# Weaving the first blocked chunk of a Fourier mixing kernel into its last plain steps

## The chip, the cores and the metric

The kernel runs on one core of a Trainium2 chip. The metric is the device time of one execution in microseconds, and before the change its median over three runs is 1843.8 us (1842.21 to 1844.92). A profile of one execution tells where the time goes; its own time is given further down, because here it is very different from the runs' median.

The engines have short names in all rows: PE is TensorE (matmuls), PEld its weight loads, DVE is VectorE, ACT is ScalarE, POOL is GpSimd and SP is SyncE, which issues nearly all DMAs here.

## The reference

```python
# x: (8, 3008, 256), w_in: (256, 2048), w_out: (2048, 256), all float32
X = np.fft.fft(x, axis=1)                   # along the 3008 positions
X = np.fft.fft(X, axis=2)                   # along the 256 features
h = X.real.reshape(24064, 256) @ w_in       # up projection
g = np.maximum(0.01 * h, h)                 # leaky relu
out = g @ w_out                             # down projection
```

## The kernel before

**The units.** The Fourier transform along the positions is done by folds (sums and differences of mirrored rows, on DVE and POOL) and matmuls with cosine and sine tables. Its result lies in `mix_sb` (a cosine and a sine part) and `nb_sb` (a separate term, "nyquist" in the code), for one *unit* at a time: a batch and a parity of the frequency, 16 units in all. The transform along the features is not done at all at run time: it is folded into the weights (`fold_w_in` makes `wf` from w_in and a table). Frequencies come in pairs of plus and minus, which differ only in the sign of the sine part. So an up projection makes a cosine and a sine product for a block of 128 of the 2048 hidden features, and DVE makes their sum and their difference.

**Two ways to compute.** The first 502 columns of unit 0 are computed as two *plain* column blocks of 251 columns each. For these there are 16 plain steps, `steps[0..15]`, each a pair (column block `j`, two feature blocks `f`). A plain step has an up half (`raised`, four matmuls into a cosine and a sine bank that `ring("up")` hands out; `activate`, four DVE operations and a leaky relu on ACT) and a down half (`down_plain`, eight matmuls into the PSUM banks that collect the output). While they run, the weights arrive and are converted from 64-bit words on DVE (`convert_on(old, new)` finishes one piece and begins the next: `w3[0]`, `w3[1]` are parts of w_in, `o4` to `o7` of w_out), and POOL adds weights to one another (`sum_weights`, 18 sums), which the second way needs.

All other columns are computed as 31 *chunks*, with a fast blocked product for the down projection: fewer matmuls, more additions. Chunk 0 is the last 250 columns of unit 0, the others have 376 or 378. A chunk has 16 *ups*. For each, ACT writes the nyquist term into the cosine bank (`Chunk.seed`), PE adds the cosine product to it and makes the sine product in a second bank (`Chunk.up`), ACT copies the cosine bank to SBUF, DVE makes sum and difference out of copy and sine bank (`Chunk.hidden`), and one up later ACT applies the leaky relu. There are two pairs of banks, `cos_ps[f % 2]` and `sin_ps[f % 2]` (the names in rows end in `a` and `b`), so that one up can begin while the other is read. After the ups come 28 sums of hidden values (`SUMS`, on POOL and partly on DVE), 26 products of four matmuls each (`PRODUCTS`, into three banks), 34 additions on DVE (`COMBINED`), and the output's stores on SP. Hidden values lie in 28 *slots* of 764 words each in `block_sb`; in the plain stage the same tile holds weights, buffers and plain hidden values.

**The order.** The order on each engine is the order in which the program issues, written out by hand. First come the plain steps: for step `at`, a conversion, then the up half of step `at`, then the down half of step `at - 2`:

```python
for at, old, new in ((8, o4, o5), (9, o5, w3[0]), (10, w3[0], w3[1]), (11, w3[1], o6),
                     (12, o6, o7), (13, o7, None), (14, None, None), (15, None, None)):
    ...
    up(*steps[at])
    if at == 11:
        fold_w_in(3 * WN, WN, w3)
    ...
    down_plain(*steps[at - 2])
    if at in SUM_WEIGHTS:          # {10: (0, 1, 2), 13: (3,)}
        ...sum_weights(last)
```

Then `rest()` makes one list of events for all chunks, sorted by a due time that counts in ups: the ups of chunk `t` at 16t + 1.2 + f, its sums at hand-written times `SUMS_AT`, its products from 16t + 18.1 on, 6.5 to an up. In step 0 to 15 of this list `start_work(r)` also issues what is left of the start: the last two down halves (r = 0, 1), the nyquist rows (r = 2) and two transforms `dft_direct` (r = 4, 7) that prepare later units. Work on the next batch comes from the generator `work()`: the load of x from step 9 (`yield 9, 0`), its folds `folds_of_x` from step 14. `wait_for_gate` lets an operation of POOL wait for an operation of DVE, where both would use SBUF at once.

The lines to know in rows of the kernel before: L880 up and L915 down matmuls of a plain step, L893 to L895 its DVE operations, L1063 seed, L1068 up matmuls, L1074 copy, L1081 sum and difference, L1329 leaky relu, L1098 a chunk's sums, L1115 its products, L576 to L595 conversions, L655 sums of weights, L934 and L936 folds of x, L693 matmuls of the transform.

## Time and profile before

| | before |
|---|---|
| median of the runs | 1843.8 us (1842.21 to 1844.92) |
| profiled execution | 3897.31 us |
| its span | 3895.5 us |
| granted clock of TensorE | 1.00 |
| PE busy | 3889.6 us |
| DVE, ACT, POOL busy | 1459.8, 1132.7, 1053.7 us |
| instructions | 27101 |
| HBM read, written | 62.12 MB, 24.72 MB |

The profiled execution took 2.11 times the median. Its rows give durations and order of every instruction; the median is what the change is measured by. Busy times are sums over the whole span. In a row of the trace the columns are: start in the span and duration in microseconds, engine, line, operation, output and inputs with their shapes; what is in brackets is idle time of the engine before the instruction, and what ended it. In a view by stretches the first column is a stretch of the span, then its length, then the busy time and the instructions of each engine, the granted clock, and what the DMA engines did.

### The profile page before, as it was taken

The page shows a single profiled execution, that of the slowest core. Times are in us where ns is not written, and L with a number is a line of the kernel's source. Part 1 is how long each engine was busy: PE and PEld are TensorE (multiplying, and loading weights), DVE is VectorE, ACT ScalarE, POOL GpSimd, SP SyncE. Part 2 cuts the span into 40 slices and gives each one's busy share as a digit, 9 for nine tenths or more (in the row PEclk, how much of TensorE's full clock was granted, in tenths as well). Part 3 has the DMA queues.
Part 4 walks back from the last instruction along what each step waited for, and adds up shares of the span by engine and source line. Part 5 has one row for each costly group of instructions (what it writes and reads, how often), then busy time and mean ns, then how long its engine had stood idle before and what let it go on. Part 6 is the DMA issues. An engine that isn't in the chain of part 4 may idle for free.

```text
span 3895.5 us, 27101 instructions
## 1 busy us (share of the span) xinstructions
PE 3889.6 (100%) x9424; PEld 2809.1 (72%) x9424; DVE 1459.8 (37%) x3212; ACT 1132.7 (29%) x2298; POOL 1053.7 (27%) x595
## 2 busy tenths in 40 slices
PE   9999999999999999999999999999999999999999
PEld 5667777777777777777777777777777777777778
DVE  4435333343334433333333433334343343333233
ACT  2234232232323323233222322223222232222220
POOL 0113222322222322232222323222223222232222
DMA  3110000000000000000001001000010000000000
GB/s 115 51 37 31 32 13 13 34 14 28 12 13 33 16 27 11 14 33 16 34 6 34 11 15 34 16 24 12 14 34 16 27 11 13 11 16 8 4 6 14
DMA packets 65897, 88.61 MB, mean 23 GB/s; under 512 B 10064, under 2 KB 53456, under 8 KB 65760
## 3 DMA queue, kind: packets, MB, share of 16 engines
q1 hardware_dynamic: 65616, 86.88, 6.9%
q8 instruction: 74, 1.21, 0.1%
q14 instruction: 63, 0.52, 0.0%
q10 hardware_dynamic: 144, 0.00, 0.0%
HBM read 62.12 MB, written 24.72 MB: 22 GB/s over the span
## 4 chain that ended last, share of the span: by engine, by line
PE 100%; DVE 0%; issue 0%; POOL 0%; DVEq 0%; POOLq 0%
PE sum_psc L1115 22%; PE sum_psa L1115 17%; PE sum_psb L1115 17%; PE sin_psb L1068 9%; PE cos_psa L1068 9%; PE sin_psa L1068 9%; PE cos_psb L1068 9%; PE dft_ps L693 2%; PE sum_psa L915 1%; PE sum_psc L915 1%; PE sum_psb L915 1%; PE dft_ps L915 1%; PE sum_psa L1359 0%; PE cos_psb L880 0%; PE cos_psa L880 0%; PE sin_psb L880 0%
## 5 line engine op out<-in xcount | busy, mean ns | idle before, releaser
L1098 POOL TENSOR_TENSOR block<-block 128x752 f32<-128x752 f32 (+2 forms) x551 | 1025.3, 1871 | 2641.9 <-DVE xt L936 559.5
L1081 DVE TENSOR_TENSOR block<-cos,sin_psa 128x376 f32<-128x376 f32 (+2 forms) x496 | 246.7, 539 | 1165.5 <-PE sin_psa L1068 1028.2
L1115 PEld LDWEIGHTS sum_psc<-block,wt 128*128 128x128 f32 x1736 | 529.3, 311 | 186.0 <-issue 171.8
L1115 PE MATMUL sum_psc<-block,wt 128*128 128x188 f32 (+2 forms) x1736 | 660.1, 552 | 0.0
L1081 DVE TENSOR_TENSOR block<-cos,sin_psb 128x376 f32<-128x376 f32 (+2 forms) x496 | 246.8, 539 | 1062.3 <-PE sin_psb L1068 1018.6
L1115 PE MATMUL sum_psa<-block,wt 128*128 128x188 f32 (+2 forms) x1736 | 640.4, 552 | 0.0
L1115 PEld LDWEIGHTS sum_psa<-block,wt 128*128 128x128 f32 x1736 | 520.4, 309 | 125.0 <-issue 108.8
L1329 ACT ACTIVATE block<-block 128x376 f32<-128x376 f32 (+4 forms) x714 | 421.7, 620 | 0.0
L1068 PE MATMUL cos_psa<-mixc,wf 128*128 128x376 f32 (+2 forms) x496 | 391.6, 906 | 0.0
L1068 PE MATMUL sin_psb<-mixs,wf 128*128 128x376 f32 (+2 forms) x496 | 391.0, 903 | 0.0
L1068 PE MATMUL cos_psb<-mixc,wf 128*128 128x376 f32 (+2 forms) x496 | 388.8, 879 | 0.0
L1068 PE MATMUL sin_psa<-mixs,wf 128*128 128x376 f32 (+2 forms) x496 | 387.4, 879 | 0.0
L1074 ACT COPY cos<-cos_psb 128x376 f32<-128x376 f32 (+2 forms) x248 | 116.5, 470 | 916.1 <-PE cos_psb L1068 916.1
L1115 PE MATMUL sum_psb<-block,wo 128*128 128x188 f32 (+2 forms) x992 | 378.0, 552 | 0.0
L1115 PEld LDWEIGHTS sum_psb<-block,wo 128*128 128x128 f32 x992 | 301.3, 310 | 101.0 <-issue 92.2
L1115 PEld LDWEIGHTS sum_psb<-block,wt 128*128 128x128 f32 x992 | 299.8, 309 | 101.4 <-issue 92.2
L1115 PE MATMUL sum_psb<-block,wt 128*128 128x188 f32 (+2 forms) x992 | 364.8, 553 | 0.0
L1074 ACT COPY cos<-cos_psa 128x376 f32<-128x376 f32 (+2 forms) x248 | 116.5, 470 | 845.0 <-PE cos_psa L1068 845.0
L1098 DVE TENSOR_TENSOR block<-block 128x752 f32<-128x752 f32 (+2 forms) x317 | 338.1, 1068 | 2.6 <-POOL block L1098 2.1
L1068 PEld LDWEIGHTS sin_psa<-mixs,wf 128*128 128x128 f32 x496 | 157.3, 317 | 176.4 <-issue 174.8
L1068 PEld LDWEIGHTS sin_psb<-mixs,wf 128*128 128x128 f32 x496 | 141.5, 285 | 191.6 <-issue 191.1
L1115 PE MATMUL sum_psc<-block,wo 128*128 128x188 f32 (+2 forms) x744 | 272.3, 550 | 0.0
(222 smaller groups left out, 2648.1 us busy)
## 6 DMA issues: line engine op xcount, KB each, us to landing
xt<-in_x_dram SPq DMA_DIRECT2D x28, 1024.0 KB, 5.5
out_dram<-part SPq DMA_DIRECT2D x176, 94.0 KB, 1.7
out_dram<-part SPq DMA_DIRECT2D x64, 94.5 KB, 1.7
tabe<-in_seq_tab_dram SPq DMA_DIRECT2D x29, 190.0 KB, 2.6
nb<-nyq_dram SPq DMA_DIRECT2D x23, 188.0 KB, 3.7
block<-in_w_in_dram SPq DMA_DIRECT2D x8, 512.0 KB, 5.5
block<-in_w_out_dram SPq DMA_DIRECT2D x8, 512.0 KB, 4.5
xt<-in_first_x_dram SPq DMA_DIRECT2D x4, 768.0 KB, 8.6
```

Of the source, the lines that this page charges most:

```text
L693: nc.tensor.matmul(o, lhsT=still, rhs=moving, start=(i == 0), stop=(i == 3), skip_group_check=True)
L915: nc.tensor.matmul(sums[j][d][:, r * n : (r + 1) * n], lhsT=wo[:, fs[h] // 4, fs[h] % 4, d], rhs=a[r][h], start=(f == 0 and r == 0 and h = ...
L1068: nc.tensor.matmul(bank[:, 0 : self.w], lhsT=wf[:, i, f * P : (f + 1) * P], rhs=columns_of(mix_sb[i], self.u, self.j, self.w), start=(i == ...
L1074: nc.scalar.copy(copy, cos[:, 0 : self.w])
L1081: nc.vector.tensor_tensor(block.row(to, g, self.n), x, y, op=op)
L1098: ins = (engine or nc.gpsimd).tensor_tensor(self.value(16 + i), xa, ya, op=ALU.add if sign > 0 else ALU.subtract)
L1115: nc.tensor.matmul(to, lhsT=weight(w)[:, g], rhs=self.value(v)[:, g], start=(first and at == 0), stop=(last and g == 3), skip_group_check= ...
L1329: nc.scalar.activation(to, to, ACT.Lrelu)
```

## The change

The change has several parts, all between plain step 8 and the second chunk.

- **Chunk 0's ups beside plain steps 12 to 15.** The loop over the plain steps ends at step 11, and `rest()` begins there. The up halves of steps 12 to 15 are issued in the event list at r = 0, 2, 4, 6, and the down halves of steps 10 to 15 in halves of four matmuls at the r of `PLAIN_DOWN`. Between them stand the ups of chunk 0. For these to have PSUM banks at the same time, the first `EARLY` = 14 ups of chunk 0 all use the pair `cos_ps[0]`, `sin_ps[0]`, and the plain steps (and the transforms at r = 9, 11, 13) use the pair `cos_ps[1]`, `sin_ps[1]`. A seed is then issued one up ahead in place of two. The leaky relu of a moved plain step is put off to the next up.
- **Narrow slots.** Hidden values of chunk 0 lie in 16 slots of 4x126 words in the first 8064 words of `block_sb`; the ordinary slots over them come free as these are dropped. The output tiles of the plain steps move to `part_sb`.
- **Conversions and sums of weights.** The conversion of o6 with o7's begin is issued at r = 0, the end of o7 at r = 2. `sum_weights(0)` and `(1)` come after step 11's up half and wait, through the gate, for the end of w3[1]'s conversion; `(2)` and `(3)` come at r = 2.
- **Other preparation.** The nyquist folds come at step 9 (before: step 14), the nyquist rows at r = 9 (2), the folds for `dft_direct` at r = 5, 7, 8, 10 (plain step 14), `dft_direct` itself at r = 11 and 13 (4 and 7). The load of x is issued at step 14 (9), its folds at step 16 (14).
- `FIRST_DOWN` = 18.1 and `FIRST_SHARE` = 1.0 have the values that stood there before.

The number and the shapes of the matmuls are the same in both kernels. The diff, cut to its core:

```diff
+EARLY = 14
+FIRST_DOWN = 18.1
+RF = 126
+FIRST_SHARE = 1.0
+DIRECT = (11, 13)
+WORK_FROM = 14
+FOLDS_FROM = 16
...
-    lay_out(part_sb, 0, (("cos", 3, WN),))
+    lay_out(part_sb, 0, (("cos", 3, WN), ("out", 2, 2 * WN)))
...
-                nc.gpsimd.tensor_tensor(weight(8 + i), weight(x), weight(y), op=ALU.add if sign > 0 else ALU.subtract)
+                wait_for_gate(nc.gpsimd.tensor_tensor(weight(8 + i), weight(x), weight(y), op=ALU.add if sign > 0 else ALU.subtract))
...
+    steps[-2:] = steps[-1], steps[-2]
...
-    def activate(j, f):
+    def activate(j, f, later=None):
...
-        nc.scalar.activation(g, g, ACT.Lrelu)
+        if later is None:
+            nc.scalar.activation(g, g, ACT.Lrelu)
+        else:
+            later.append([g])
...
-            self.free = set(range(SLOTS))
+            self.under = {SLOTS + i: {4 * RF * i // SS, (4 * RF * (i + 1) - 1) // SS} for i in range(16)}
+            self.free = set(range(SLOTS)) - set().union(*self.under.values())
...
+        def half(self, f):
+            return 0 if self is every[0] and f < EARLY else f % 2
+
         def seed(self, f):
-            nc.scalar.activation(cos_ps[f % 2][:, 0 : self.w], columns_of(nb_sb, self.u, self.j, self.w), ACT.Copy, scale=wn[:, f : f + 1])
+            nc.scalar.activation(cos_ps[self.half(f)][:, 0 : self.w], columns_of(nb_sb, self.u, self.j, self.w), ACT.Copy, scale=wn[:, f : f + 1])
 
         def up(self, f):
-            cos, sin = cos_ps[f % 2], sin_ps[f % 2]
+            cos, sin = cos_ps[self.half(f)], sin_ps[self.half(f)]
...
-        yield 9, 0
+        yield WORK_FROM, 0
         load_x(1, 0)
-        yield step_of(1, -2), 0
+        yield FOLDS_FROM, 0
         folds_of_x(0)
...
-        rings["dft"] = [0, [misc_ps, *sums_ps]]
+        rings["up"] = [0, [cos_ps[1], sin_ps[1]]]
...
+        def seed_next(at):
+            if at < EARLY:
+                seed(at + 1)
+            if at + 2 > EARLY:
+                seed(at + 2)
...
-    SUM_WEIGHTS = {10: (0, 1, 2), 13: (3,)}
+    PLAIN_UP = {0: 12, 2: 13, 4: 14, 6: 15}
+    PLAIN_DOWN = {0: (10, 0), 1: (10, 1), 3: (11, 0), 4: (11, 1), 5: (12, 0), 7: (12, 1), 8: (13, 0), 9: (13, 1),
+                  10: (14, 0), 12: (14, 1), 15: (15, 0), 17: (15, 1)}
 
     def start_work(r):
-        if r < 2:
-            down_plain(*steps[14 + r])
+        if r == 0:
+            convert_on(o6, o7)
+        if r in PLAIN_UP:
+            raised(*steps[PLAIN_UP[r]])
+            activate(*steps[PLAIN_UP[r]], later=waiting)
+        if r in PLAIN_DOWN:
+            at, half = PLAIN_DOWN[r]
+            down_plain(*steps[at], halves=(half,))
         if r == 2:
+            convert_on(o7, None)
+            sum_weights(2)
+            sum_weights(3)
+        if r in (5, 7):
+            part = (r - 5) // 2
+            fold_halves(t, part, 0, slice(0, 2 * FI))
+            evens.append(Direct(t[:, part, 0, :, part * P : (part + 1) * P], part, even_tables[part], 0))
+        if r in (8, 10):
+            evens[(r - 8) // 2].fold_odd(t[:, (r - 8) // 2, 1, 0:2, 0:P])
+        if r == 9:
+            rings["dft"] = rings["up"]
             nyq_t = nyquist_tile()
...
-        if r in (4, 7):
-            dft_direct((r - 4) // 3)
+        if r in DIRECT:
+            dft_direct(DIRECT.index(r))
...
-            for at, old, new in ((8, o4, o5), (9, o5, w3[0]), (10, w3[0], w3[1]), (11, w3[1], o6), (12, o6, o7), (13, o7, None), (14, None, None), (15, None, None)):
-                if old is not None:
-                    convert_on(old, new)
+            for at, old, new in ((8, o4, o5), (9, o5, w3[0]), (10, w3[0], w3[1]), (11, w3[1], o6)):
+                done = convert_on(old, new)
...
                 if at == 11:
                     fold_w_in(3 * WN, WN, w3)
+                    gate.append(done)
+                    sum_weights(0)
+                    sum_weights(1)
...
-                if at in SUM_WEIGHTS:
-                    for last in SUM_WEIGHTS[at]:
-                        sum_weights(last)
-                if at == 14:
+                if at == 9:
                     fold_nyquist(0)
                     nyq = Rows(nya[:, 0], [nyz], 0, 0)
...
-                    for part in range(2):
-                        fold_halves(t, part, 0, slice(0, 2 * FI))
-                        evens.append(Direct(t[:, part, 0, :, part * P : (part + 1) * P], part, even_tables[part], 0))
-                    for part in range(2):
-                        evens[part].fold_odd(t[:, part, 1, 0:2, 0:P])
             rest()
```

More of the change, by code (lines that the diff above doesn't have):

```diff
@@ L587, in end @@
             if not self.f64:
-                nc.vector.tensor_copy(self.dst, self.raw)
-                return
+                return nc.vector.tensor_copy(self.dst, self.raw)
             hi = self.word(I32, 1)
@@ L594, in end @@
             v.scalar_tensor_tensor(power_i, in0=hi, scalar=-(2**31), in1=power_i, op0=ALU.bitwise_and, op1=ALU.bitwise_or)
-            v.scalar_tensor_tensor(man, in0=man, scalar=2.0**-20, in1=power, op0=ALU.mult, op1=ALU.mult)
+            return v.scalar_tensor_tensor(man, in0=man, scalar=2.0**-20, in1=power, op0=ALU.mult, op1=ALU.mult)
     parts = []
@@ L610, in convert_on @@
             new.begin()
-        old.end()
+        return old.end()
     def load_w_in(f0, n, blocks=(0, 1)):
@@ L903, in out_tile @@
     def out_tile():
-        return ring("o")[:, 0 : 4 * CW].rearrange("p (a n) -> p a n", a=2)
+        return ring("out")[:, 0 : 4 * CW].rearrange("p (a n) -> p a n", a=2)
     def down_plain(j, f, halves=(0, 1)):
@@ L1009, in drop @@
         def drop(self, i):
-            self.free.add(i)
+            if i in self.under:
+                freed = self.under.pop(i)
+                self.free |= freed - set().union(*self.under.values())
+            else:
+                self.free.add(i)
         def place(self, i, n):
+            if i >= SLOTS:
+                return block_sb[:, (i - SLOTS) * 4 * RF : (i - SLOTS + 1) * 4 * RF].rearrange("p (g n) -> p g n", g=4)[:, :, 0:n]
             return block_sb[:, i * SS : i * SS + 4 * RS].rearrange("p (g n) -> p g n", g=4)[:, :, 0:n]
         def row(self, r, g, n):
+            if r[0] >= SLOTS:
+                all_of = block_sb[:, 0 : 64 * RF].rearrange("p (i n) -> p i n", n=4 * RF)
+                return all_of[:, r[0] - SLOTS : r[-1] + 1 - SLOTS, g * RF : g * RF + n]
             all_of = block_sb.rearrange("p (i n) -> p i n", n=SS)
@@ L1071, in up @@
             if g == 0:
-                self.at.update(zip(range(4 * k, 4 * k + 4), block.take_four()))
+                self.at.update(zip(range(4 * k, 4 * k + 4), block.take_four() if self is not every[0] else range(SLOTS + 4 * k, SLOTS + 4 * k + 4)))
             copy = cos_sb[:, f % 2, 0 : self.w]
@@ L1243, in work @@
                 yield from transform(u + 1)
-    every = []
+    every, waiting = [], []
     def rest():
@@ L1257, in rest @@
             for m in range(4 * len(PRODUCTS)):
-                events.append((16 * t + DOWN_FROM + m / PER_STEP, 2, t, m))
+                events.append((16 * t + (DOWN_FROM if t else FIRST_DOWN) + m / PER_STEP, 2, t, m))
         for r in range(16 * count + 18):
@@ L1269, in seed @@
                 every[ups[at][0]].seed(ups[at][1])
-        us = [0.0, 0.0]
+        def seed_next(at):
[3 more added lines that the diff above has]
+                seed(at + 2)
+        us, now = [0.0, 0.0], [1.0]
         def some(pool):
-            us[pool], us[1 - pool] = min(us[pool], 0.3) + (ON_VECTOR, ON_POOL)[pool], us[1 - pool] - 100.0
+            us[pool], us[1 - pool] = min(us[pool], 0.3) + (ON_VECTOR, ON_POOL)[pool] * now[0], us[1 - pool] - 100.0
             for part in every:
@@ L1295, in go_on @@
                 empty = -1
-        after, waiting = [0], []
+        after = [0]
         seed(0)
-        seed(1)
         for _, kind, t, i in events:
             if kind == 0:
-                if t == 0:
-                    start_work(i)
-                elif t < count:
+                start_work(16 * t + i)
+                now[0] = FIRST_SHARE if 16 * t + i < 34 else 1.0
+                if 0 < t < count:
                     rings["dft"] = [0, [misc_ps]]
@@ L1325, in rest @@
                 made = part.up(i)
-                seed(16 * t + i + 2)
+                seed_next(16 * t + i)
                 folds.emit_copies()
@@ L1503, in tile_fnet_leaky_relu @@
                 up(*steps[at])
-                if at == 11:
-                    fold_w_in(3 * WN, WN, w3)
-                if at == 8:
-                    down_plain(*steps[at - 2], halves=(1,))
-                else:
-                    down_plain(*steps[at - 2])
-                if at in SUM_WEIGHTS:
-                    for last in SUM_WEIGHTS[at]:
-                        sum_weights(last)
-                if at == 14:
+                if at == 9:
                     fold_nyquist(0)
@@ L1518, in tile_fnet_leaky_relu @@
                     nyq_of.append(nyq)
-                    for part in range(2):
-                        fold_halves(t, part, 0, slice(0, 2 * FI))
-                        evens.append(Direct(t[:, part, 0, :, part * P : (part + 1) * P], part, even_tables[part], 0))
-                    for part in range(2):
-                        evens[part].fold_odd(t[:, part, 1, 0:2, 0:P])
+                if at == 11:
+                    fold_w_in(3 * WN, WN, w3)
+                    gate.append(done)
+                    sum_weights(0)
+                    sum_weights(1)
+                if at == 8:
+                    down_plain(*steps[at - 2], halves=(1,))
+                else:
+                    down_plain(*steps[at - 2])
             rest()
```

## The prediction

> **What bounds the kernel now.** I read the page's first two parts, then stretches of the stage that the change touches, then single engines in time. The page says that TensorE is all:

> ```profile
> span 3895.5 us, 27101 instructions
> ...
> PE 3889.6 (100%) x9424; PEld 2809.1 (72%) x9424; DVE 1459.8 (37%) x3212; ACT 1132.7 (29%) x2298; POOL 1053.7 (27%) x595
> ```

> The profiled execution took 3897.3 us: its span of 3895.5 and 1.8 around it. The runs' median is 1843.8, 0.473 of that. So the first question is which engine is slow in the profile. This row and the next start 3.63 us apart, for four matmuls of 251 columns (each stands as two records):

> ```profile
> 241.60 3.79 PE L915 MATMUL dft_ps<-block,wo 128*128 128x251 f32 x8
> 245.23 1.16 PE L1068 MATMUL cos_psa<-mixc,wf 128*128 128x250 f32 x2
> ```

> That is 3.6 ns a column. The program has 4712 matmuls; the shapes of the PE groups add up to 1,061,690 columns, and the median divided by them is 1.74 ns, with every stall in it. [...] By the row, TensorE never waits and a change of order is worth nothing: 3897 stays 3897. [...] I take 1.667 ns for TensorE and the trace's durations for the rest. Stretches: steps 9 to 11, steps 12 to 15 with the last downs ("P"), the first chunk's ups ("D"), the second chunk's ups ("E"):

> ```profile
> core 0: us, PE busy (x) PEld busy (x) DVE busy (x) ACT busy (x) POOL busy (x), PEclk, DMA share, GB/s
> 127.70:186.60 58.90, 58.90 (x114) 33.88 (x112) 22.33 (x36) 13.52 (x18) 9.45 (x7) 1.00 0.08 21
> 186.60:245.20 58.60, 58.60 (x129) 38.89 (x128) 12.96 (x25) 7.41 (x13) 15.74 (x21) 1.00 0.03 9
> 245.20:288.40 43.20, 43.20 (x106) 28.50 (x105) 19.08 (x57) 23.53 (x54) 0.68 (x1) 1.00 0.21 70
> 288.40:330.00 41.60, 41.60 (x119) 29.78 (x118) 21.20 (x39) 19.90 (x38) 14.38 (x11) 1.00 0.18 61
> ```

> P has 64 matmuls of 251 columns: 26.8 us of TensorE against 13.0 of DVE and 7.4 of ACT. D has 11,794 columns, 19.7 us, against 23.5 of ACT: there ACT is the bound. In P TensorE is the bound and ACT idles; the change lays the two over each other. How ACT fills D:

> ```profile
> 280.36 0.37 ACT L1074 COPY cos<-cos_psb 128x250 f32<-128x250 f32 x1 [0.34 <-PE cos_psb L1068]
> 280.76 0.47 ACT L1063 ACTIVATE cos_psb<-nb,wn 128x250 f32<-128x250 f32 x1
> 281.17 0.60 ACT L1329 ACTIVATE block<-block 128x500 f32<-128x500 f32 x1
> ...
> 285.41 0.62 ACT L1329 ACTIVATE block<-block 128x500 f32<-128x500 f32 x1
> 285.94 0.34 ACT L1074 COPY cos<-cos_psa 128x250 f32<-128x250 f32 x1
> ```

> From start to start a copy takes 0.40, a seed 0.41, a leaky relu 0.53: 1.34 us an up, where TensorE needs 500 columns, 0.83 us.

> **The change part by part.**

> **1. First chunk's ups among the last plain steps.** Before: P 26.8. Then D: ups 0 to 7 stand among the nyquist rows and two butterflies (3,794 columns, 6.3 us, beside 8 ups of 0.83), and with the last output copy and the butterflies' adds on DVE ahead of some ups' adds, ACT comes to the copy of up 8 at 15. Then it goes on by 1.34: six ups, a fold copy (0.51), the copy of up 14 and E's first seed (0.9), so the first up of E starts at 24.5. (ACT's busy sum of 23.5 and 0.7 at the start give nearly the same.) P and D are 51.3 us.
> After: the same columns, 27,858, are 46.4 us, with ACT at 31 and DVE at 32 beneath. But the first 14 ups share one pair of banks. Between two ups there is mostly half a down step (4x251 columns, 1.67 us) or a plain up (1.67). The next cos matmul needs copy and seed, 0.15 + 0.40 + 0.47 = 1.0 us after the last one; the next sin matmul needs DVE's pair of adds (0.74). Both fit into 1.67. Going up by up I find three places where they don't: at step 2 DVE stands in the end of o7's conversion (0.61 + 0.71 + 0.65) before the adds of up 1, TensorE waits 1.3; after the nyquist rows (1.5 us on DVE) 0.2; between ups 12 and 13, where nothing lies between, 0.6 and 0.4. Sum 2.5, so 48.9. Gain 2.4. The 0.15 from a matmul's end to its reader isn't in this trace; 0 would give 0.5 us more, 0.4 would stall half of the ups by 0.2, 1.5 less.

> **2. Folds of x two steps later.** Before, DVE enters E with a queue:

> ```profile
> 292.23 1.00 DVE L1081 TENSOR_TENSOR block<-cos,sin_psa 128x378 f32<-128x378 f32 x2
> 293.14 0.68 DVE L934 TENSOR_TENSOR xt<-xt,dft_ps 128x512 f32<-128x512 f32 x1
> 293.74 1.42 DVE L1098 TENSOR_TENSOR block<-block 128x500 f32<-128x500 f32 x1
> ```

> Even here nothing lies between them. At full speed the first fold copy is there 23.0 us into D; then three folds, two sums and a fold (0.60 each) and two ups' adds (0.74 each), with 0.1 of waiting, bring up 15's adds to 28.2. E's second up needs that bank and could have gone on at 26.6 (24.5, a first up of 756 columns and a product before it, its own cos half): 1.6 us are lost. After, five of the fold operations (0.60 each, start to start) come behind the adds, and two halves of a down step have given DVE and POOL time: that loss is gone, gain 1.6. They come back in E: by the built orders DVE has 41.7 us under the 16 ups of E where it had 39.3 (512 elements 0.60, 250 elements 0.33), and TensorE 39.0. From the seventh up the two orders nearly agree. I take 0.7 lost of the 2.4 (0 to 2.4), because the next three ups are lighter.
> The x loads, issued at step 14 instead of 9, wait on SP behind two output stores. They may start 41.2 us in and are first needed by ACT at 48.4: 7.2 us for what the trace shows landing in 5.2. Cost 0; without that cover ACT stands still with the output copies behind it, for which the first product waits.

> **3. Sums of weights behind the conversions.** Before, seven sums on POOL (from 146.68, 9.4 us) meet the conversion of w3[0]:

> ```profile
> 149.99 0.68 DVE L893 TENSOR_TENSOR block<-part,sin_psa 128x502 f32<-128x502 f32 x1 [0.89 <-PE sin_psa L880]
> ...
> 152.10 1.49 DVE L576 TENSOR_SCALAR block<-block 128x512 int32<-128x512 int32 x1
> ...
> 162.78 0.42 DVE L576 TENSOR_SCALAR wo<-block 128x512 int32<-128x512 int32 x1
> ```

> Four DVE instructions of that conversion take 5.5 us (from 151.17 to 156.71) where the next one's take 2.0 (162.17 to 164.17). At full speed, counted from the end of up 9: its adds 1.35, the conversion 2.6 + 3.5, step 10's activation 2.05, w3[1]'s conversion 2.6, together 12.1. TensorE has 24 matmuls of 251 (10.0) and the first half of a fold (0.85) until it needs w3[1]: at 10.85. It waits 1.3. After, the sums wait for o6's start and w3[1]'s end; the gain is 1.3. [...] But TensorE doesn't wait for o6: step 12's activation begins at 1.6 instead of 1.0 and the next plain up in its bank comes at 5.85. So 1.3 stays, from 0 to 1.7. Later sums (11 of 1.27) come under adds out of PSUM, and two folds of 0.95 that may double; their readers have 0.5 us to spare. Behind them POOL's first chunk sum is free at 25 us and needed at 45.

> **4. Taken at nothing.** Narrow slots: the same operations and elements (from -0.1 to +0.1 us each, I take 0). Nyquist folds moved up to step 9 on POOL, 2.5 us, under POOL's long idle time; without it ACT's four 0.29 us turns would hold back a conversion. Output tiles in part: the same copies and stores, of which the chunk's adds no longer have to wait.

> Sum: 2.4 + 1.6 - 0.7 + 1.3 = 4.6 us. 1843.8 - 4.6 = 1839.2. In the profiled execution, where TensorE hides all this, I expect no change from 3897.3.

> **The rivals.** *A: more than that.* If ACT and DVE wait longer for each other in D than I counted (0.2 us for each of 16 ups is 3), and the interleaved order has no stall (2.5), the gain is 10: 1834. For it: D has nothing to hide a wait. Against: its ACT rows follow each other closely. *B: one bank pair in place of two.* If the way from cos matmul through copy and seed, or from sin through the adds, takes over 2.1 us (1.67 and the rest of an up), each of 14 ups stalls: at 2.8, by 0.7, 9.8 us, so slower by 5: 1849. Decisive is whether DVE has a plain activation (2.2 us) ahead of the adds at steps 2, 4 and 6. Against: the way is 1.0 us where nothing is in it. *C: hidden anyway.* The unprofiled chain doesn't stand at these places, or E takes the gain back through DVE (2.4): 1842.

> **How the numbers follow.** Forecast (gain 3 to 7) 0.58, A 0.18, C 0.15, B 0.09. A measurement of this kernel tells about 0.2%, 3.7 us, from no change. The forecast lies partly below that: faster 0.70, same 0.21, slower 0.09. The range, 1832.5 to 1843.5, leaves out B and the end of A.

> **What would show it.** In the profile after: the first chunk's ups between downs, with ACT's copies no longer close together; the conversions of w3 at 0.42 and 0.69 with o6's at 1.4 and more; no chunk sum of 1.42 on DVE at E's start; POOL's second group of sums without a gap behind o7. Wrong: TensorE idle before the sin matmuls of ups 1 to 7 (B), or ACT waiting for the x load. A time above 1843.8 would mean B; one under 1834 that D cost more than ACT's sum.

## The result, and the profile after

The changed kernel takes 1834.53 us (median of four runs, 1831.76 to 1834.64) against 1844.27 for the kernel before: a ratio of 0.9945, 95% interval 0.9928 to 0.9963, or 9.7 us less. The forecast of 1839.2 had the direction and its range held the time, but the gain is twice the forecast 4.6, outside the 3 to 7 that the forecast gave itself.

The head of the page after:

```profile
span 1832.8 us, 27088 instructions
...
PE 1818.5 (99%) x9424; PEld 1547.3 (84%) x9424; DVE 1546.2 (84%) x3212; ACT 1124.6 (61%) x2298; POOL 1101.7 (60%) x595
```

This execution took 1834.63 us, as the timed runs do: TensorE, busy for 1818.5 us, is not slowed here as it was in the profile before (3889.6). So one profile can't be compared with the other. The kernel before was therefore profiled again (first experiment), and that execution took 1842.16 us, as its timed runs do. The two can be laid side by side, stage by stage, from the starts of the same matmuls in the two timelines:

| stretch | before (again) | after | difference | forecast |
|---|---|---|---|---|
| start to plain step 12's first matmul | 97.63 | 91.24 | -6.39 | -1.3 (part 3) |
| from there to the second chunk's first up | 52.43 | 49.71 | -2.72 | -2.4 (part 1) |
| second and third chunk | 103.13 | 102.04 | -1.09 | -0.9 (part 2) |
| fourth chunk to the last one's first up | 1488.73 | 1488.72 | 0.0 | 0 |
| from there to the end of the span | 98.42 | 101.13 | +2.71 | 0 |

Two of the three parts are where the forecast had them, to 0.3 us. The third, the sums of weights, brought five times its term. And the end, which the change doesn't touch, gave 2.7 us back in this pair of executions. The experiments are about these two.

The same stretches, as the view by stretches shows them (before again, then after; columns as in the prediction):

```profile
core 0: us, PE busy (x) PEld busy (x) DVE busy (x) ACT busy (x) POOL busy (x), PEclk, DMA share, GB/s
85.03:94.22 9.19, 6.34 (x8) 2.48 (x9) 8.44 (x16) 4.00 (x5) 0.29 (x1) 0.63 0.07 28
97.63:125.59 27.96, 27.45 (x129) 24.13 (x128) 17.98 (x25) 7.35 (x13) 17.36 (x21) 1.00 0.04 14
125.59:150.06 24.47, 22.47 (x106) 16.39 (x104) 17.37 (x54) 20.65 (x51) 0.00 (x0) 1.00 0.37 131
```

```profile
84.40:87.83 3.43, 3.43 (x9) 1.52 (x8) 3.33 (x7) 1.38 (x3) 3.13 (x3) 1.00 0.00 0
91.24:140.95 49.71, 48.07 (x233) 41.37 (x232) 36.40 (x84) 28.83 (x61) 22.19 (x17) 1.00 0.18 62
```

The first line of each is the fold of w3 in step 11: four matmuls of 512 columns. Before, it lasts 9.19 us with TensorE busy for 6.34, at a mean granted clock of 0.63. After, it lasts 3.43, without a gap, at 1.00. The other lines are the stages P and D of the prediction, and what became of them: TensorE waits 0.5 and 2.0 us in the two, and 1.6 in the merged one.

TensorE in the fold, in the kernel before, again:

```profile
85.03 1.13 PE L629 MATMUL cos_psb<-block 128*128 128x512 f32 x2 [0.71 <-DVE part L889]
89.00 2.07 PE L629 MATMUL cos_psb<-block 128*128 128x512 f32 x2 [2.85 <-DVE block L595]
90.87 3.52 PE L629 MATMUL sin_psb<-block 128*128 128x512 f32 x4
```

The second matmul waits for the end of w3[1]'s conversion (L595). What DVE does ahead of the fold there:

```profile
74.81 0.86 DVE L889 SCALAR_TENSOR_TENSOR part<-nb,wn,cos_psa 128x251 f32<-128x251 f32 x2
75.77 0.68 DVE L893 TENSOR_TENSOR block<-part,sin_psa 128x502 f32<-128x502 f32 x1
76.37 0.67 DVE L894 TENSOR_TENSOR block<-part,sin_psa 128x502 f32<-128x502 f32 x1
76.95 1.08 DVE L584 SCALAR_TENSOR_TENSOR block<-block 128x512 f32<-128x512 uint32 x1
77.95 1.49 DVE L576 TENSOR_SCALAR block<-block 128x512 int32<-128x512 int32 x1
79.36 1.49 DVE L577 TENSOR_SCALAR block<-block 128x512 int32<-128x512 int32 x1
80.78 1.75 DVE L594 SCALAR_TENSOR_TENSOR block<-block 128x512 int32<-128x512 int32 x1
82.57 1.64 DVE L595 SCALAR_TENSOR_TENSOR block<-block 128x512 f32<-128x512 f32 x1
84.13 0.85 DVE L889 SCALAR_TENSOR_TENSOR part<-nb,wn,cos_psb 128x251 f32<-128x251 f32 x2
```

And in the kernel after:

```profile
77.18 0.68 DVE L591 SCALAR_TENSOR_TENSOR block<-block 128x512 f32<-128x512 uint32 x1
77.78 0.42 DVE L583 TENSOR_SCALAR block<-block 128x512 int32<-128x512 int32 x1
78.12 0.42 DVE L584 TENSOR_SCALAR block<-block 128x512 int32<-128x512 int32 x1
78.45 0.68 DVE L600 SCALAR_TENSOR_TENSOR block<-block 128x512 int32<-128x512 int32 x1
79.17 0.69 DVE L601 SCALAR_TENSOR_TENSOR block<-block 128x512 f32<-128x512 f32 x1
...
86.68 1.07 DVE L591 SCALAR_TENSOR_TENSOR wo<-block,wo 128x512 f32<-128x512 uint32 x1
87.67 1.50 DVE L583 TENSOR_SCALAR wo<-block 128x512 int32<-128x512 int32 x1
```

The conversion of w3[0] takes 7.2 us from 76.95 where it now takes 2.6 from 77.18: all five instructions of it were drawn out by POOL's sums, not four. The last two rows show that the clash has moved to o6, as the prediction said, and TensorE has no gap there.

### The profile page after: what moved, and what is told of

Same layout as the page of the kernel before. It is cut to its first block, busy times and chain, and to the rows that moved or that the text cites. A ratio compares the mean times of both kernels' runs of the same rounds, so it can differ in the third digit from the quotient of the medians.

```text
span 1832.8 us, 27088 instructions
## 1 busy us (share of the span) xinstructions
PE 1818.5 (99%) x9424; PEld 1547.3 (84%) x9424; DVE 1546.2 (84%) x3212; ACT 1124.6 (61%) x2298; POOL 1101.7 (60%) x595
## 4 chain that ended last, share of the span: by engine, by line
PE 96%; DVE 2%; POOL 1%; issue 1%; POOLq 0%; ACT 0%; DVEq 0%
PE sum_psc L1140 21%; PE sum_psa L1140 17%; PE sum_psb L1140 16%; PE cos_psa L1093 9%; PE sin_psa L1093 8%; PE cos_psb L1093 8%; PE sin_psb L1093 8%; PE dft_ps L699 3%; PE sum_psa L925 1%; PE dft_ps L925 1%; PE sum_psb L925 1%; PE sum_psc L925 1%; DVE part L1184 1%; PE sum_psa L1410 1%; POOL block L1123 1%
## 5 line engine op out<-in xcount | busy, mean ns | idle before, releaser
L1360 ACT ACTIVATE block<-block 128x376 f32<-128x376 f32 (+5 forms) x718 | 426.4, 623 | 3.2 <-DVE block L1106 2.5
L1140 PEld LDWEIGHTS sum_psc<-block,wt 128*128 128x128 f32 x1736 | 291.2, 190 | 47.1 <-issue 1.8
L1140 PE MATMUL sum_psc<-block,wt 128*128 128x188 f32 (+2 forms) x1736 | 329.2, 322 | 1.7 <-DVE part L1184 1.7
L1140 PE MATMUL sum_psa<-block,wt 128*128 128x188 f32 (+2 forms) x1736 | 312.8, 321 | 0.4 <-POOL block L1123 0.4
L1140 PEld LDWEIGHTS sum_psa<-block,wt 128*128 128x128 f32 x1736 | 283.4, 189 | 23.5 <-POOL block L1123 0.7
L1093 PE MATMUL cos_psa<-mixc,wf 128*128 128x376 f32 (+2 forms) x510 | 199.8, 473 | 0.5 <-ACT cos_psa L1088 0.5
L1184 DVE TENSOR_TENSOR part<-part 128x188 f32<-128x188 f32 (+2 forms) x465 | 189.8, 445 | 2.8 <-ACT part L1156 1.0
L1093 PE MATMUL sin_psb<-mixs,wf 128*128 128x376 f32 (+2 forms) x482 | 191.5, 479 | 0.0
L1093 PE MATMUL cos_psb<-mixc,wf 128*128 128x376 f32 (+2 forms) x482 | 191.4, 478 | 0.0
L1140 PE MATMUL sum_psb<-block,wo 128*128 128x188 f32 (+2 forms) x992 | 187.6, 321 | 0.0
```

The lines of the kernel that those rows point to most:

```text
L1093: nc.tensor.matmul(bank[:, 0 : self.w], lhsT=wf[:, i, f * P : (f + 1) * P], rhs=columns_of(mix_sb[i], self.u, self.j, self.w), start=(i == ...
L1140: nc.tensor.matmul(to, lhsT=weight(w)[:, g], rhs=self.value(v)[:, g], start=(first and at == 0), stop=(last and g == 3), skip_group_check= ...
L1184: ins = nc.vector.tensor_tensor(part_of[self.copy[v]][:, 0:n], xa, ya, op=ALU.add if sign > 0 else ALU.subtract)
L1360: nc.scalar.activation(to, to, ACT.Lrelu)
```

## The experiments

Times are medians, ratios go against runs of the kernel before on the same chip. Where the trace gives the start of the fourth chunk, that is used as well: from there to the last chunk all kernels run alike, to 0.02 us, so it shows what a change of the start is worth without the end's spread. It is a reading of one execution each, and the clock in the fold moves it: with the fold unchanged it lay at 253.19 in the first experiment and at 252.29 in the ninth.

**1. The kernel before, again.** Nothing is changed.

> The kernel before, unchanged, for a profile in which TensorE runs as fast as in the timed runs, and for the spread of a comparison of a kernel with itself. Theory as predicted: from the first matmul of plain step 12 to the first up of the second chunk it takes 51.3 us (the changed kernel's profile shows 49.7 for the same 27,858 columns), and the rest of the 9.7 us lies in the conversions (1.3) and the second chunk. Rival A, waits between ACT and DVE in the first chunk's ups: 55 us or more, with TensorE idle before most of the ups from the eighth on. Ratio to before 1.000 within 0.002.

1843.53 us, ratio 0.9999 (0.9991 to 1.0008), runs from 1841.23 to 1845.56. From step 12 to the second chunk it takes 52.43 us, close to the 51.3 of the forecast; the first chunk's ups take 24.47 where 24.5 was worked out. Rival A's waits in the first chunk are not there, though its time (1834) is nearly what was measured. The missing gain lies ahead of this stage.

**2. The sums of weights alone, in the kernel before.**

```diff
-    SUM_WEIGHTS = {10: (0, 1, 2), 13: (3,)}
+    SUM_WEIGHTS = {11: (0, 1), 13: (2, 3)}
...
                 if at == 11:
                     fold_w_in(3 * WN, WN, w3)
+                    gate.append(done)
```

(`done` is the last instruction of w3[1]'s conversion, and the sums wait for the gate, as in the change.)

> The kernel before with one part of the change alone: the sums of weights of the first two groups come after step 11's up half and wait for the end of w3[1]'s conversion, the other two come after o7's. Theory as predicted: 1.3 us faster (0 to 1.7), and the conversion of w3[0] in 2 to 3 us where it took 5.5. Rival: the clash only moves to o6, 0. Rival: most of the 9.7 us sits here, 4 us or more.

1837.68 us, ratio 0.9969 (0.9958 to 0.9981): 5.8 us, the second rival. The fourth chunk starts 5.42 us earlier. Plain step 12 starts 6.6 us earlier (91.00), and 1.2 are lost in one place behind it: the second group of sums now meets more of the folds of step 14 on DVE (two folds of 768 elements take 3.76 us from 104.39, 3.44 before; four of 128 take 5.17 from 108.07, 4.37 before), step 15's activation is late, and TensorE waits 1.72 us for it (0.51 before). The changed kernel spreads these folds over r = 5 to 10.

**3. x's folds later, alone, in the kernel before.**

```diff
-        yield 9, 0
+        yield 14, 0
         load_x(1, 0)
-        yield step_of(1, -2), 0
+        yield 16, 0
```

> The kernel before with x's load issued at step 14 in place of 9 and its folds from step 16 in place of 14, nothing else. Theory as predicted: 1.6 us gained before the second chunk and 0.7 lost in it, so 0.9 faster (-0.8 to 1.6). Rival: the folds collide with the first chunk's additions wherever they lie (in the changed kernel TensorE waits 1.66 and 0.56 us for those, at 183 and 188 us): no faster, or up to 1 us slower.

1842.28 us, ratio 0.9992 (0.9984 to 1.0000): the medians alone hardly tell this from no change. The fourth chunk starts 0.90 us earlier. That is the forecast's 0.9 as a sum, but not place by place: step 12 starts 0.39 later here, and TensorE still waits 0.85 us in the second chunk's second up (0.96 before), so the 1.6 ahead of it does not come from the later folds alone.

**4. The sums put back, in the changed kernel.**

```diff
-                    gate.append(done)
-                    sum_weights(0)
-                    sum_weights(1)
...
+                if at == 10:
+                    for last in (0, 1, 2):
+                        sum_weights(last)
```

> The changed kernel with the sums of weights put back: groups 0 to 2 at step 10 without a wait, group 3 behind o7. Theory as predicted: 1.3 us slower than the changed kernel, so 8.4 faster than before; the conversion of w3[0] takes 5.5 us again and the weights' fold at step 11 waits for w3[1]. Rival, most of the gain sits in the sums: 4 us or more slower than the changed kernel. Rival, hidden: as fast as the changed kernel.

1842.75 us, ratio 0.9994 (0.9986 to 1.0003). The whole gain is gone: the fourth chunk starts 8.5 us later than in the changed kernel, more than the 6.4 of the table, because the clash takes a worse form here. The nyquist folds, now at step 9, push POOL's first sum from 74.97 to 80.02, and at 82.05 DVE begins with w3[1]:

```profile
82.05 7.13 DVE L591 SCALAR_TENSOR_TENSOR block<-block 128x512 f32<-128x512 uint32 x1
89.11 0.41 DVE L583 TENSOR_SCALAR wo<-block 128x512 int32<-128x512 int32 x1
```

One instruction of 0.68 us lasts 7.13, until POOL's last sum has ended (88.6). TensorE stands for 5.72 us ahead of the fold's second matmul.

**5. The sums at their new place, without the wait.**

```diff
-                    gate.append(done)
```

> The changed kernel with the sums of weights at their new place in the order but without the wait for w3[1]'s conversion. Theory: POOL has nothing else ahead of them and their weights are long there, so they run where they ran before, beside the conversions of w3, and TensorE waits and loses its clock as with the sums put back: 1842 to 1843. Rival, the place in the order is what counts: 1834.5, as the changed kernel.

1840.45 us, ratio 0.9988 (0.9981 to 0.9994); the fourth chunk starts 8.2 us later than in the changed kernel. The median lies 1.5 below what was expected, but the same row appears (7.13 us at 82.09) and the fold waits 5.71 us. A place in the order of POOL holds nothing back; the wait does.

**6. The wait kept, the clock held.** In the kernel before, TensorE gets work for the time that it waits for w3[1] (`warm` is 6 for w3, else 0). The product of the extra matmuls is not used.

```diff
+                    if w == 1 and a == 0:
+                        for _ in range(warm):
+                            nc.tensor.matmul(sin_ps[1][:, 0:256], lhsT=feat_sb[:, 0, 0:P], rhs=made[0].dst[:, 0:256], start=True, stop=True)
```

> The kernel before with six extra matmuls of 256 columns (their product is not used) in the fold of w3, between the half that needs w3[0] and the half that needs w3[1]: TensorE still waits for w3[1] in effect, but not idle. In the profile of before at full speed the fold takes 9.19 us (85.03 to 94.22) where four matmuls of 512 columns at 1.687 ns take 3.46: 0.71 and 2.85 are idle, and the granted clock is 0.5 from 87.33 to 94.16. Theory: the clock fell because TensorE stood idle, so the extra matmuls keep it at 1.00, the fold's last three matmuls take 2.6 us from the end of w3[1]'s conversion at 88.9, and the kernel is 2.6 us faster (2 to 3) although the conversion ends no earlier. Rival: the slow matmuls have another cause (SBUF contention with POOL and DVE): no faster, 0 to 0.5 slower.

1840.80 us, ratio 0.9988 (0.9980 to 0.9996); the fourth chunk starts 1.99 us earlier although w3[1]'s conversion ends 0.6 us later (89.46, 88.87 before). From that end to the end of the fold it takes 2.8 us, before 5.35. The clock in the view by stretches, before again and then with the extra matmuls:

```profile
83.92:87.33 3.41, 1.53 (x4) 0.30 (x3) 3.31 (x8) 0.95 (x1) 1.40 (x1) 1.00 0.39 140
87.33:94.16 6.83, 5.16 (x6) 2.19 (x7) 6.19 (x12) 3.05 (x5) 0.00 (x0) 0.50 0.00 1
```

```profile
83.92:87.33 3.41, 2.42 (x9) 1.12 (x8) 3.31 (x6) 0.36 (x1) 2.00 (x2) 1.00 0.54 154
87.33:92.28 4.95, 4.95 (x19) 3.13 (x18) 4.81 (x11) 2.31 (x4) 0.00 (x0) 1.00 0.00 0
```

A stretch of 3.41 us in which TensorE is busy for 1.53 is followed by 6.83 us at half the clock (0.50), and three of the fold's four matmuls fall into these (5.16 us busy); with the extra matmuls (2.42 busy in the same stretch) the clock stays at 1.00. So in this profile the stall was worth 3.6 us of waiting (0.71 and 2.85) and some 2.5 of slow matmuls after it.

**7. One pair of banks, without cover.** In the kernel before, the first 14 ups of the first chunk use one pair (`half` and `seed_next` as in the change), at their old place.

> The kernel before, where the first chunk's first 14 ups use one pair of PSUM banks in place of two, at the old place behind the plain steps (nothing lies between most of them). Theory as predicted: from a cos matmul's end through copy and seed to the next cos matmul it takes 1.0 us, so an up takes 0.42 + 1.05 to 1.1 = about 1.5 where it took 1.30: 0.2 for each of the ups without another matmul between them, 1 to 2.5 us slower in all. Rival B: the way is over 2.1 us, an up takes 2.5 or more, 9 us or more slower.

1849.76 us, ratio 1.0036 (1.0022 to 1.0050). The first chunk takes 30.53 us, 6.1 more than before; neither forecast holds. The timeline of TensorE there:

```profile
147.89 0.69 PE L1071 MATMUL cos_psa<-mixc,wf 128*128 128x250 f32 x2 [0.54 <-ACT cos_psa L1066]
148.41 0.58 PE L1071 MATMUL sin_psa<-mixs,wf 128*128 128x250 f32 x2
149.54 0.69 PE L1071 MATMUL cos_psa<-mixc,wf 128*128 128x250 f32 x2 [0.54 <-ACT cos_psa L1066]
```

And ACT between the two cos matmuls:

```profile
148.61 0.37 ACT L1077 COPY cos<-cos_psa 128x250 f32<-128x250 f32 x1 [0.24 <-PE cos_psa L1071]
149.01 0.47 ACT L1066 ACTIVATE cos_psa<-nb,wn 128x250 f32<-128x250 f32 x1
```

An up takes 1.65 us (147.89 to 149.54) where it took 1.30: 0.35 each, not 0.2. Where ups had followed each other every 0.84 us (133.14 and 133.98 in the first experiment), the loss is 0.8 (134.49 and 136.14 here); the forecast took 1.30 for all. Counted with 0.42 us for the cos matmul's 250 columns (the step from one to the next where nothing waits, 133.14 to 133.56 in the first experiment), it ends at 148.31, the copy begins 0.30 after that, copy and seed take 0.87, and the next matmul starts 0.06 later. The way is 1.2 us, not the 1.0 of the prediction, whose 0.15 from a matmul's end to its reader, the author's assumption, is 0.30 by this count. In the changed kernel it matters only where nothing of 1.67 us lies between two ups.

**8. The end's clock, in the changed kernel.** The product of the extra matmuls is not used.

```diff
+                if t == count - 1 and i == 16:
+                    for _ in range(8):
+                        nc.tensor.matmul(misc_ps[:, 0:256], lhsT=wf[:, 0, 0:P], rhs=wf[:, 0, 0:256], start=True, stop=True)
                 every[t].product(*divmod(i, 4))
```

> The changed kernel with eight extra matmuls of 256 columns into a free bank (product not used) in the last chunk, before the fifth product, where TensorE waits 3.56 us for POOL (1792.1 to 1795.7) and the clock is 0.5 from 1795.03 to 1801.86 in the profile. Theory: the clock stays at 1.00, 3.4 us of matmuls at half speed are won back, and the runs lie closer together: 1831.3, 3.2 faster than the changed kernel where the clock had fallen and 0 where it had not (its runs were 1831.76 to 1834.64). Rival: the last chain runs over POOL and DVE, not TensorE: no change.

1831.74 us, 1831.59 to 1832.24, ratio 0.9938 (0.9926 to 0.9951): 2.8 us faster than the changed kernel, and at the fastest of its runs. The changed kernel, ahead of the wait, in it and after:

```profile
1790.67 1.44 PE L1140 MATMUL sum_psb<-block,wo 128*128 128x188 f32 x8
1795.66 2.87 PE L1140 MATMUL sum_psc<-block,wo 128*128 128x188 f32 x8 [3.56 <-POOL block L1123]
1798.33 4.45 PE L1140 MATMUL sum_psc<-block,wt 128*128 128x188 f32 x16
1802.62 1.44 PE L1140 MATMUL sum_psc<-block,wo 128*128 128x188 f32 x8
```

The same eight records take 1.44 us, then 2.87, then 1.44 again. The granted clock is 0.50 from 1795.03 to 1801.86 and 1.00 around that; with the extra matmuls it is 1.00 from 1791.60 to 1801.00.

**9. The same extra matmuls in the kernel before.**

> The kernel before with the same eight extra matmuls in the last chunk (product not used). Its runs spread from 1840.8 to 1845.5, those of the changed kernel with the extra matmuls from 1831.6 to 1832.2. Theory: the spread is the clock in the last wait for POOL, in some executions at 0.5 and in some not: the runs lie within 1 us, near the fast end, 1841.5, and the changed kernel's gain without this is 9.8 us. Rival: the spread comes from the start, where the clock also falls in the fold of w3: it stays, 1840 to 1845.

1841.74 us, 1841.09 to 1842.60, ratio 0.9995 (0.9987 to 1.0003). The upper part of the spread is gone, and 1.5 us of it are left, so the end's clock was most of it. The rest fits the fold's: in this profile the clock was at half there for 3.42 us (89.80 to 93.22) and step 12 starts at 96.73, in that of before for 6.83 us and at 97.63. No run here shows it for each execution. With the end's clock held in both kernels, the change is worth 10.0 us (1841.74 - 1831.74, on two chips whose medians of the kernel before are 1842.96 and 1842.87); the fourth chunk's start moves by 10.20 in the pair of the table and by 9.66 in this one.

**10 and 11. Four sums from DVE to POOL, alone and with the extra matmuls.**

```diff
-                every[t].sum(i, nc.vector if i in BY_VECTOR or ...
+                every[t].sum(i, nc.vector if i in BY_VECTOR and not (t == 0 and i in (16, 17, 21, 25)) or ...
```

> The changed kernel with four of the first chunk's sums (16, 17, 21 and 25 of the list) on POOL in place of DVE. In the changed kernel DVE has hardly a gap from 141 to 192 us, and TensorE waits 1.66 and 0.56 us for its additions at 183 and 188 us; POOL idles more than half of that time. Theory: DVE is the bound of the second chunk's ups in the changed kernel; four sums of 0.60 us less, and it comes 2.4 us earlier to the additions that TensorE waits for: 2.2 us faster than the changed kernel, second chunk's start to third chunk's start 42.4 us in place of 44.6. Rival: the wait comes from POOL or from the two engines' turns (sums on POOL run while DVE stands at the gate, or slow DVE's own from 0.67 to 1.3 and more): no gain, or up to 2 us lost.

> The changed kernel with the four sums on POOL and with the eight extra matmuls of the last chunk that keep the clock up. Theory: the two gains add, 3 to 5 us faster than the changed kernel, about 1829.5. Rival: the sums bring nothing or a loss on POOL, 1831.7 or more, as with the extra matmuls alone.

1833.71 us (ratio 0.9948, 0.9936 to 0.9961) and 1832.32 us (0.9938, 0.9925 to 0.9952). The rival holds: the second chunk takes 45.2 us in place of 44.6, and the fourth chunk starts 0.43 and 0.56 us later than in the changed kernel. The 0.8 us in the first median lie at the end: from the fourth chunk's start on its profile takes 1588.5 us, the changed kernel's 1589.9, and its mean granted clock over the span is 0.999 where the changed kernel's is 0.998. The waits of TensorE stay at 1.66 and 0.56 us. A row of DVE in the changed kernel, 6 us ahead of the first of these waits:

```profile
177.43 0.55 DVE L1106 TENSOR_TENSOR block<-cos,sin_psa 128x378 f32<-128x378 f32 x1 [0.91 <-POOL block L1123]
```

DVE waits for a POOL sum before it can write the second half of an up; from there to the additions that TensorE waits for it has no gap. With more sums on POOL there is a second such wait, of 0.98 us. Here a sum given to POOL saved DVE 0.6 us (179.69 to 180.28 in the changed kernel), and four of them brought it one such wait more.

**12. The two stalls of the merged stage.** Extra matmuls as in experiment 8, and

```diff
-EARLY = 14
+EARLY = 13
...
-        if r == 2:
+        if r == 3:
             convert_on(o7, None)
```

> The changed kernel with the eight extra matmuls of the last chunk, with the end of o7's conversion (and the sums of weights behind it) at r = 3 in place of 2, and with EARLY = 13, so that up 13 uses the other pair of banks. In the changed kernel TensorE waits in the merged stage at two places: 1.10 us before the sin matmul of up 2, whose bank's additions stand on DVE behind o7's conversion, and 0.54 before the cos matmul of up 13, whose seed comes late behind up 12. Theory: these are the price of one pair of banks, both go, 1.6 us faster than with the extra matmuls alone: 1830.1, and the stage from the first of plain step 12's matmuls to the second chunk takes 48.1 us in place of 49.7. Rival: o7's conversion only meets the next up's additions (1.1 us later elsewhere) or delays w_out's last piece: 1831.7 or more.

1830.13 us, 1830.10 to 1830.80, ratio 0.9933 (0.9921 to 0.9946), the fastest version here. Its stage from step 12 to the second chunk takes 48.08 us. What the waits ahead of it had been, in the changed kernel, and the one that is left here:

```profile
103.09 0.69 PE L1093 MATMUL sin_psa<-mixs,wf 128*128 128x250 f32 x2 [1.10 <-DVE block L1106]
...
134.78 0.69 PE L1093 MATMUL cos_psa<-mixc,wf 128*128 128x250 f32 x2 [0.54 <-ACT cos_psa L1088]
```

```profile
133.65 0.69 PE L1093 MATMUL cos_psb<-mixc,wf 128*128 128x250 f32 x2 [0.41 <-ACT cos_psb L1088]
```

The first is gone with o7's conversion behind the additions. The other bank pair did little for the second: the seed of up 13 is issued behind up 12's copy (132.85), though ACT stood idle for 1.39 us ahead of that copy.

## Why the prediction was right, and where it was not

**TensorE's rate: right.** The prediction took 1.667 ns a column, its author's assumption, against the 3.6 of the profile; the median gave it only a bound, 1.74 with every stall. In the changed kernel's profile two matmuls of 251 columns take 0.85 us from start to start (97.17 to 98.02), which is 1.69, and two of the fold's matmuls of 512 take 1.71 (84.40 to 86.11), which is 1.67. But the step "in the profiled execution I expect no change from 3897.3" was wrong: the profile of the changed kernel took 1834.63 us. The trace of the slow profile has no record of the clock at all, so the granted 1.00 in its views is no reading. At a granted clock of 0.50 a column took 3.55 ns (four matmuls of 188 columns in 2.67 us, 1795.66 to 1798.33 in experiment 8), and 3.33 in the last three of the four (1796.45 to 1798.33). So a clock at half throughout would explain most of the 3.6, an estimate from these two figures; it is not shown, and why that execution was slow stays open.

**Part 1, the overlay: right.** 52.4 to 49.7 against 51.3 to 48.9. Of the three stalls counted there, two are seen, 1.10 for 1.3 and 0.54 for 1.0, and the 0.2 behind the nyquist rows is not. The way through one pair is 1.2 us in place of 1.0, and the half down steps (1.69 us, 135.87 to 137.56 in the changed kernel, for the forecast's 1.67) cover the one as the other. This is what kept rival B away: uncovered, the pair costs 6.1 us.

**Part 2, folds of x: right in sum, both terms somewhat larger.** 1.09 for 0.9. Counted from the second chunk's first up, its third comes 1.80 us earlier than before (at 4.36 us, before at 6.16), which is the term of 1.6. The fifteenth comes 2.93 earlier, because TensorE had also waited 0.47 us for POOL there. Then 1.8 are lost again where 0.7 were forecast: ahead of the last products of the second chunk TensorE waits 1.66 and 0.56 us for additions on DVE, before 0.67. That is within the 0 to 2.4 that was allowed for.

**Part 3, sums of weights: the mechanism right, the size wrong, 6.4 for 1.3.** This is the failed step, in two terms.
- "Together 12.1": DVE's time from the end of up 9 to the end of w3[1]'s conversion is 14.9 (73.97 to 88.87). DVE was still 0.84 us in o5's conversion, with the whole activation of step 9 behind it (2.14, taken as 1.35), and the fifth instruction of w3[0]'s conversion was drawn out as well (7.2, taken as 6.1). So TensorE waited 3.6 us, not 1.3. The prediction had read the chain in a profile with TensorE at less than half its rate, where DVE waits for it (0.89 us ahead of the row at 149.99) and has no backlog.
- "It waits 1.3" counted the wait alone. During this wait the clock fell to half, which no row of the slow profile could show: some 2.5 us more (experiment 6). The prediction saw 1.00 in all stretches, put the clock at nothing, and did not ask what a longer wait would do to it. In the first experiment's profile it fell after 3.41 us in which TensorE was busy for 1.53, or 45%, and stayed at half for 6.83.

**The clash with POOL's sums moved, and cost nothing there.** In the changed kernel it fell on o6's conversion (1.50 us at 87.67 where 0.42 is usual), and TensorE had no gap there. DVE's additions with an input in PSUM kept their time beside the sums: 0.68 and 0.67 us at 75.77 and 76.37 in the first experiment, 0.68 and 0.67 at 89.83 and 90.42, where no sum runs.

**The rivals.** A's 1834 was hit for another reason: its waits in the first chunk did not exist. That the range held the time is in part luck: it reached that far for A's sake, and what filled the gap was part 3. "Hidden anyway" was wrong. The end's +2.7 in one pair of profiles was in no case of the prediction: it is the clock in the last wait for POOL, which fell to 0.50 for 6.83 us in the changed kernel's profile (wait 3.56) and stayed at 1.00 in the first experiment's (wait 3.40).

## What to carry to other kernels

Where an engine must deliver just in time to TensorE, price its delay twice: the wait, and the matmuls behind it at half the clock. Here the clock fell after stretches of 3.41 us in which TensorE was busy for 0.35 to 1.53 us, and stayed up after ones with 1.49, 1.93 and 2.42. Keep long series of POOL operations on SBUF away from DVE operations on SBUF that TensorE waits for (one of 0.68 us lasted 7.13 in experiments 4 and 5), with a wait and not with a place in the order, and let the clash fall where nobody waits. Where a wait can't be removed, matmuls that nobody needs can be issued into it: here eight at the end and six at the start held the clock at 1.00, and brought 2.8 and 2.0 us.
